# A grouped 1x1 convolution on one core: an in-place ring of five slots of 104 columns in place of four of 128

## The chip, the core and the metric

The kernel runs on one core of one Trainium2 chip. The metric is the device time of the program in microseconds (us). A core has a matmul engine (TensorE, PE in the profile; its weight loads are shown apart as PEld), VectorE (DVE), ScalarE (ACT), GpSimd (POOL) and SyncE (SP), each with an instruction queue of its own, and 16 DMA engines that all transfers share. SyncE and ScalarE issue transfers that the hardware unrolls; GpSimd issues transfers that its software unrolls.

## The reference

A 1x1 grouped convolution over 512 x 512 pixels of 192 channels: four groups of 48 channels, each with its own 48 x 48 matrix. Input, weights and output are bf16.

```
x: [1, 512, 512, 192]   w: [1, 1, 4, 48, 48]
xg  = x.reshape(1, 512, 512, 4, 48)
out = einsum('bhwgc,gcd->bhwgd', xg, w[0, 0]).reshape(1, 512, 512, 192)
```

So each pixel's 192 values are multiplied by a block-diagonal 192 x 192 matrix. 100.7 MB are read and 100.7 MB written.

## The kernel before

**Layout.** A "column" is one pixel in each of the 128 partitions, 384 bytes per partition. The input comes into a ring in SBUF, `ring`, of `COLS` columns (512 here, four slots of `SLOT` = 128). The work is in place: results are written over the inputs, and the slot is then stored to the output from the ring. A "group" is 4 columns, a "pair" two groups. There are 529 groups, in 265 pairs (the last has one group).

**Pieces.** `plan_pieces` cuts the image into pieces. The first slot comes in four pieces of growing size (`HEAD`), the others in one piece of `SLOT` columns each; the last slot has what is left, 68 columns here. Two slots, those whose numbers are in `SHARED_AT`, end in a shared piece of 64 columns (`WIDE`) that uses only 60 of the 128 rows and is loaded and stored by GpSimd, in row ranges that leave out one of the 16 DMA engines. Before such transfers GpSimd issues tiny ones (`cur`) that move its place among the engines.

**Who does what.**

- SyncE loads the pieces in order (line 248). Before each it waits until the stores of the columns that the piece takes over have landed (`wait_free`). After the first piece it issues the load of the weights (line 250).
- GpSimd waits for each piece's landing and then adds the piece's pairs to the semaphore `ready` (line 233). It also issues the shared pieces' loads, two pieces ahead, and their stores.
- TensorE first spreads the weights into the block-diagonal matrix `wt` by 10 small matmuls (line 262). Then, for every pair, it transposes the two groups (12 transposes, line 285, into `xT_ps`) and, one pair behind, multiplies the transposed groups by `wt` (12 matmuls, line 299, into `o_ps`). It waits on `ready` at the pairs where a piece may begin. The loop over pairs is a hardware loop whose body is two slots (`LOOP` groups, 64 here); the ring address of each group comes from registers, six a group, computed from a base that depends on the turn (line 269). What is left after whole turns is written out straight.
- VectorE copies each pair's transposed data from PSUM to SBUF (line 336).
- ScalarE copies each group's result from PSUM back over the group's columns in the ring (line 362) and issues the store of a piece as soon as its last group and one more are done (line 356). The stores of the last three slots are cut in halves, and the last slot's store in `LAST_PARTS`.

**Order.** Each engine's order is written out by hand; nothing is planned by cost. PSUM has four banks for transposed groups (`NXP`) and four for results (`NOB`), SBUF two buffers for transposed pairs (`NXS`).

Of the kernel before, what the change touches and what calls it, by code (L numbers as in the profile page):

```python
# [22 lines left out]
ESHIFT = 112  # L23
ECOLS = 272

SLOT = 128
COLS = 4 * SLOT
COL = 2 * C
HEAD = (8, 24, 32, 64)
LATE = 3  # L30
LAST_PARTS = (28, 16, 12, 12)
LOOP = 2 * SLOT // 4
SHARED_AT = (4, 10)
RING = 16766
SYNC, POOL = 0, 1
WIDE = 64
# [27 lines left out]
class Piece:  # L64

    def __init__(self, i, slot, g0, size, shares, pix):
        self.i, self.slot, self.size = i, slot, size
        self.at = 4 * g0 % COLS
        self.g0, self.g1 = g0, g0 + size // 4
# [5 lines left out]
        self.pix_end = pix  # L75
        assert size % 4 == 0 and self.at + size <= COLS

# [4 lines left out]
def plan_pieces(npix):  # L82
    few = sum(rows * cols for _, rows, _, cols, _ in SHARED)
    at = list(SHARED_AT)
    if npix < len(at) * few + 128 * SLOT * (1 + at[-1]):
        at = []
# [3 lines left out]
    while cols:  # L90
        if n in at:
            parts = [(SLOT - WIDE, None), (WIDE, SHARED)]
        elif n == 0 and cols >= SLOT:
            parts = [(s, None) for s in HEAD]
        else:
            parts = [(min(SLOT, cols), None)]
        for s, shares in parts:
# [8 lines left out]
def bass_standalone__grouped__vision_kernel(nc, x, w, out):  # L106
# [9 lines left out]
    LP = LOOP // 2  # L116
# [5 lines left out]
    wv = w.rearrange("a b g c d -> c (a b g) d")  # L122

    def groups(pair):
        return range(2 * pair, min(2 * pair + 2, NG))

    def span(c0, c1, r0=0, r1=128):
        return ring[r0:r1, c0 * COL:c1 * COL].bitcast(BF16)
# [13 lines left out]
    for p in pieces:  # L142
        late = pieces[-1].slot - p.slot
        half = p.size // 8 * 4
        parts = (p.size,)
        if p is pieces[-1] and p.size == sum(LAST_PARTS):
            parts = LAST_PARTS
        elif p.full and late < LATE and half:
            parts = (p.size - half, half)
        c = 0  # L150
# [7 lines left out]
    with ExitStack() as es:  # L158
        block = es.enter_context(nc.Block())
        ring = es.enter_context(nc.sbuf_tensor("ring", [128, COLS * COL], U8))  # L160
        xT_sb = [es.enter_context(nc.sbuf_tensor(f"xT_sb{i}", [128, 4 * UC], BF16)) for i in range(NXS)]
        ident = es.enter_context(nc.sbuf_tensor("ident", [128, 128], BF16))
        esel = es.enter_context(nc.sbuf_tensor("esel", [CG, ECOLS], BF16))
        w_sb = es.enter_context(nc.sbuf_tensor("w_sb", [CG, GROUPS, CG], BF16))
# [4 lines left out]
        def sem(name):  # L169
            return es.enter_context(nc.semaphore(name))  # L170
# [7 lines left out]
        w_sem, id_sem, e_sem, wb_sem, wc_sem = (sem(s) for s in ("w_sem", "id_sem", "e_sem", "wb_sem", "wc_sem"))  # L178
# [4 lines left out]
        def columns(g):  # L183
            c = 4 * g % COLS
            return span(c, c + 4)

        def wait_stored(wq, i):
            p = stores[i][0]
            wq.wait(st_sem[i], 16 * len(p.on(SYNC)))
            if p in pooled:  # L190
                wq.wait(ps_sem[p], pool_val[p])

        def wait_free(wq, p):
            lap = COLS // 4
            for i in sorted({store_of[g - lap] for g in range(p.g0, p.g1) if g >= lap}):
                wait_stored(wq, i)
# [45 lines left out]
        @block.sync  # L242
        def _(sp):
            wq = Waiter(sp)
            for p in pieces:
                wait_free(wq, p)
                for _, dram, sbuf in transfers(xf, p, SYNC):
                    sp.dma_start(sbuf, dram).then_inc(ld_sem[p.i], 16)  # L248
                if p.i == 0:
                    sp.dma_start(w_sb[:], wv).then_inc(w_sem, 16)  # L250

        @block.tensor
        def _(pe):

            def build_weights():
                pe.wait_ge(e_sem, 1)
                pe.wait_ge(w_sem, 16)
                last = None
                for (tc, r, g, c0_) in WBLOCKS:
                    s0 = ESHIFT - r  # L260
                    col = WOFF[tc] + c0_
                    last = pe.matmul(o_ps[:, NOB - 1, col:col + CG], lhsT=esel[:, s0:s0 + 128],  # L262
                                     rhs=w_sb[:, g, :], start=True, stop=True, skip_group_check=True)
                last.then_inc(wb_sem, 1)

            def addresses(base, g):
                regs = [pe.alloc_register(f"at{g}_{i}") for i in range(6)]
                for i, r in enumerate(regs):
                    pe.reg_add(r, base, RING + 4 * g * COL + i * 256)
                return [pe.snap(r, donate=True, min_val=RING, max_val=RING + COLS * COL - 256,  # L270
                                guaranteed_mod_val=0, out_of_modulus=2) - RING for r in regs]

            def transposes(j, gs, base=None):
                if j % LP in starts:
                    n = min((s - j) % LP or LP for s in starts)
                    pe.wait_ge(ready, min(j + n, NP - first[0]))
                last = None
                for g in gs:
                    if base is None:
                        ats = [4 * g % COLS * COL + i * 256 for i in range(6)]  # L280
                    else:
                        ats = addresses(base, g % LOOP)
                    for i, at in enumerate(ats):
                        xs = ring[:, bass.ds(at, 256)].bitcast(BF16)
                        last = pe.transpose(xT_ps[:, g % NXP, i * 128:(i + 1) * 128], xs, ident[:])  # L285
                last.then_inc(t_left, 1)

            def matmuls(j, gs):
                pe.wait_ge(e_left, j + 1)
                for g in gs:  # L290
                    xs = xT_sb[j % NXS][:, g % 2 * 2 * UC:(g % 2 + 1) * 2 * UC]
                    pe.wait_ge(o_left, g + 1)
                    last = None
                    for ul in range(2):
                        v = 2 * g + ul
                        for tc in range(3):
                            i = ul * 3 + tc
                            c0_, c1_ = COLR[tc]
                            last = pe.matmul(o_ps[:, v % NOB, c0_:c1_], lhsT=xs[:, i * 128:(i + 1) * 128],  # L299
                                             rhs=wt[:, WOFF[tc]:WOFF[tc] + (c1_ - c0_)],  # L300
                                             start=(tc == 0), stop=(tc == 2), skip_group_check=True)
                    last.then_inc(mm_done, 1)

            first = [0]
            build_weights()
            pe.wait_ge(id_sem, 1)
            pe.sem_inc(o_left, 2)
            transposes(0, groups(0))
            pe.wait_ge(wc_sem, 1)
            if turns_of_loop:  # L310
                with pe.Fori(0, turns_of_loop) as turn:
                    here = pe.snap((turn & 1) * (LOOP * 4 * COL))
                    there = pe.snap(((turn + 1) & 1) * (LOOP * 4 * COL))
                    for j in range(LP):
                        transposes(j + 1, range(2 * j + 2, 2 * j + 4), here if j + 1 < LP else there)
                        matmuls(j, range(2 * j, 2 * j + 2))
                    pe.sem_inc(ready, -LP)
                    pe.sem_inc(e_left, -LP)
                    pe.sem_inc(o_left, -LOOP)
            first[0] = LP * turns_of_loop  # L320
            for j in range(NP - first[0]):
                if j + 1 < NP - first[0]:
                    transposes(j + 1, groups(first[0] + j + 1))
                matmuls(j, [g - 2 * first[0] for g in groups(first[0] + j)])
# [22 lines left out]
        @block.scalar  # L347
        def _(act):
            wq = Waiter(act)
            todo = list(stores)  # L350

            def store():
                i = len(stores) - len(todo)
                p, c0, c1, g1 = todo.pop(0)
                for _, dram, sbuf in transfers(of, p, SYNC, c0, c1):
                    act.dma_start(dram, sbuf).then_inc(st_sem[i], 16)

            for g in range(NG):
                wq.wait(mm_done, g + 1)
                v = 2 * g  # L360
                dst = columns(g).rearrange("p (u c) -> p u c", u=2)
                act.copy(dst, o_ps[:, v % NOB:v % NOB + 2, 0:UC]).then_inc(o_left, 1)  # L362
                while todo and todo[0][3] < g:
                    store()
            while todo:
                act.wait_ge(o_left, todo[0][3] - LOOP * turns_of_loop + 2)
                store()
            for i in range(len(stores)):
                wait_stored(wq, i)
# [28 lines left out]
```

## Time and profile before

| | |
|---|---|
| Three timed runs | 478.95, 482.16, 483.46 us; median 482.16 |
| The profiled execution | 477.98 us, span 476.3 us |
| Granted TensorE clock, mean | 0.979 |
| TensorE busy | 438.8 us (92%), its weight loads 397.6 us (83%) |
| ScalarE busy | 399.0 us (84%) |
| VectorE busy | 254.0 us (53%) |
| GpSimd busy | 10.0 us (2%) |
| DMA | 7565 packets, 201.52 MB, mean 423 GB/s over the span |
| Loads by SyncE | 20, of 384 to 6144 KB |
| Stores by ScalarE | 25, of 384 to 6144 KB |
| Chain that ended last | DMA 57%, TensorE 38% |

The profile is of one execution. Times inside it count from the first instruction of the program, so the span is a little less than the execution's own time. "DMA share" is the mean busy share of the 16 DMA engines. The first wait for the weights' load ends at 4.24 us; the transposes of the first pair start at 4.73 us and those of the second, which need the second piece, at 9.32 us.

### The profile page before, as it was taken

The numbers are of one execution on the slowest core, as the hardware profiler recorded it, in microseconds if no ns is written. First come the engines' busy times: TensorE is split into PE (matmuls) and PEld (weight loads), VectorE is DVE, ScalarE is ACT, GpSimd is POOL, SyncE is SP. The second block draws the span as 40 slices with busy tenths as digits, with TensorE's granted clock in tenths as the row PEclk, the third lists the DMA queues.
The fourth block names the chain that finished last, engine by engine and source line by source line (L and its number), as shares of the span: only waits on it lengthen the run. The fifth ranks groups of instructions, "written<-read, shape, count | busy, mean of one in ns | idle before, by whom it ended". The sixth has DMA issues, their size and how long they took to land.

```text
span 476.3 us, 14542 instructions
## 1 busy us (share of the span) xinstructions
PE 438.8 (92%) x6358; PEld 397.6 (83%) x6358; DVE 254.0 (53%) x266; ACT 399.0 (84%) x530; POOL 10.0 (2%) x23
## 2 busy tenths in 40 slices
PE   3999889999999999999799999999899998989993
PEld 3988778898888989888798889889798977979982
DVE  2555545655556555565355655555555553545651
ACT  1888879999899989999599998989898995968993
POOL 1000000100001000000010000010000000000000
PEclk9999999999999999999799999999999998989997
DMA  8999999999999999999999999999999999999997
GB/s 285 436 421 441 433 418 427 440 431 444 425 433 429 420 431 436 452 413 450 421 434 425 414 433 425 438 429 423 438 436 433 434 429 433 433 424 421 431 412 292
DMA packets 7565, 201.52 MB, mean 423 GB/s; under 512 B 1553, under 2 KB 1553, under 8 KB 2193
## 3 DMA queue, kind: packets, MB, share of 16 engines
q1 hardware_dynamic: 3088, 97.73, 48.1%
q10 hardware_dynamic: 3600, 97.72, 47.8%
q0 software_dynamic: 864, 5.91, 3.0%
q8 instruction: 8, 0.13, 0.1%
q14 instruction: 5, 0.03, 0.0%
HBM read 100.69 MB, written 100.66 MB: 423 GB/s over the span
## 4 chain that ended last, share of the span: by engine, by line
DMA 57%; PE 38%; issue 2%; ACT 1%; SPq 0%; POOL 0%; POOLq 0%
DMA ring<-in_x_dram 32%; DMA out_dram<-ring 24%; PE o_ps L299 22%; PE xT_ps L285 16%; ACT ring L362 1%; SPq L248 0%; POOL cur L218 0%; POOL out_dram L220 0%; SPq L250 0%; POOLq L233 0%; SPq L54 0%
## 5 line engine op out<-in xcount | busy, mean ns | idle before, releaser
L362 ACT CAST ring<-o_ps 128x768 bf16<-128x768 f32 x529 | 397.7, 802 | 69.5 <-PE o_ps L299 61.7
L336 DVE COPY xT_sb<-xT_ps 128x1536 bf16<-128x1536 bf16 x265 | 253.3, 956 | 208.0 <-PE xT_ps L285 208.0
L299 PE MATMUL o_ps<-wt,xT_sb 128*128 128x144 bf16 (+1 forms) x3174 | 296.5, 235 | 8.1 <-issue 3.6
L299 PEld LDWEIGHTS o_ps<-wt,xT_sb 128*128 128x128 bf16 x3174 | 215.2, 99 | 46.3 <-ACT ring L362 29.9
L285 PE MATMUL xT_ps<-ident,ring 128*128 128x128 bf16 x3174 | 225.0, 221 | 17.4 <-POOLq L233 14.6
L285 PEld LDWEIGHTS xT_ps<-ident,ring 128*128 (+1 forms) x3174 | 193.6, 99 | 20.2 <-issue 19.9
L218 POOL DMA_DIRECT2D cur<-in_x_dram x7 | 4.2, 596 | 306.5 <-DMA out_dram<-ring 169.4
L262 PE MATMUL o_ps<-w_sb,esel 48*128 48x48 bf16 x10 | 0.6, 210 | 4.2 <-DMA w_sb<-in_w_dram 4.2
L262 PEld LDWEIGHTS o_ps<-w_sb,esel 48*128 48x128 bf16 x10 | 0.5, 112 | 4.2 <-issue 4.2
L330 DVE CAST wt<-o_ps 128x480 bf16<-128x480 f32 x1 | 0.7, 658 | 4.8 <-PE o_ps L262 4.8
L220 POOL DMA_DIRECT2D ring<-in_x_dram x4 | 2.3, 582 | 0.0
L220 POOL DMA_DIRECT2D out_dram<-ring x4 | 2.3, 576 | 0.0
L362 ACT ACT_TABLE_LOAD x1 | 1.3, 1283 | 0.8 <-PEq L383 0.8
L204 POOL TENSOR_SCALAR_AFFINE_SELECT esel<-esel 48x272 bf16<-48x272 bf16 x1 | 0.4, 402 | 0.0
L201 POOL MEMSET esel<- 48x272 bf16 x1 | 0.3, 317 | 0.3 <-POOLq L383 0.3
L208 POOL TENSOR_SCALAR_AFFINE_SELECT ident<-ident 128x128 bf16<-128x128 bf16 x1 | 0.3, 282 | 0.0
L202 POOL MEMSET ident<- 128x128 bf16 x1 | 0.2, 198 | 0.0
L383 POOL MEMSET const-float32-0.0<- 128x1 f32 x1 | 0.1, 98 | 0.3 <-issue 0.3
L383 POOL MEMSET const-bfloat16-1.0<- 128x1 bf16 x1 | 0.1, 101 | 0.0
L383 POOL MEMSET const-uint8-127<- 128x1 uint8 x1 | 0.1, 101 | 0.0
L383 POOL MEMSET const-float32-1.0<- 128x1 f32 x1 | 0.1, 98 | 0.0
## 6 DMA issues: line engine op xcount, KB each, us to landing
ring<-in_x_dram SPq DMA_DIRECT2D x13, 6144.0 KB, 39.7
out_dram<-ring ACTq DMA_DIRECT2D x11, 6144.0 KB, 35.0
out_dram<-ring ACTq DMA_DIRECT2D x7, 3072.0 KB, 31.8
ring<-in_x_dram SPq DMA_DIRECT2D x3, 3072.0 KB, 22.1
ring<-in_x_dram SPq DMA_DIRECT2D x1, 3264.0 KB, 34.0
ring<-in_x_dram POOLq DMA_DIRECT2D x2, 1056.0 KB, 25.4
out_dram<-ring POOLq DMA_DIRECT2D x2, 1056.0 KB, 28.9
ring<-in_x_dram SPq DMA_DIRECT2D x1, 1536.0 KB, 11.0
```

The lines of the kernel that those rows point to most:

```text
L201: gp.memset(esel[:], 1.0).then_inc(p0_sem, 1)
L204: gp.affine_select(out=esel[:], in_=esel[:], pattern=[[-1, ECOLS]], compare_op=AluOpType.is_equal, fill=0.0, base=ESHIFT, channel_multipli ...
L208: gp.affine_select(out=ident[:], in_=ident[:], pattern=[[-1, 128]], compare_op=AluOpType.is_equal, fill=0.0, base=0, channel_multiplier=1) ...
L218: gp.dma_start(cur[0:n, turns[0]], few).then_inc(cur_sem, 16)
L220: gp.dma_start(*((sbuf, dram) if inward else (dram, sbuf))).then_inc(done, 16)
L262: last = pe.matmul(o_ps[:, NOB - 1, col:col + CG], lhsT=esel[:, s0:s0 + 128], rhs=w_sb[:, g, :], start=True, stop=True, skip_group_check=True)
L285: last = pe.transpose(xT_ps[:, g % NXP, i * 128:(i + 1) * 128], xs, ident[:])
L299: last = pe.matmul(o_ps[:, v % NOB, c0_:c1_], lhsT=xs[:, i * 128:(i + 1) * 128], rhs=wt[:, WOFF[tc]:WOFF[tc] + (c1_ - c0_)], start=(tc == ...
L330: dve.tensor_copy(wt[:], o_ps[:, NOB - 1, 0:WCOLS]).then_inc(wc_sem, 1)
L336: dve.tensor_copy(xT_sb[pair % NXS][:, 0:n * 2 * UC].rearrange("p (g c) -> p g c", g=n), xT_ps[:, b0:b0 + n, 0:2 * UC]).then_inc(e_left, 1)
L362: act.copy(dst, o_ps[:, v % NOB:v % NOB + 2, 0:UC]).then_inc(o_left, 1)
L383: nc = _bacc.Bacc("TRN2", target_bir_lowering=False, num_devices=1)
```

## The change

- `SLOT` goes from 128 to 104 and the ring from four slots to five, so from 512 to 520 columns. There are then 20 full slots and a last one of 36 columns.
- `HEAD`'s last piece goes from 64 to 40 columns, the last slot's store parts are 16, 12 and 8 columns, and the shared pieces stand in slots 6 and 13 instead of 4 and 10.
- TensorE's loop body is still two slots, now 52 groups. As two slots no longer divide the ring evenly, a turn's base isn't one of two values: three slot bases (the third for the pair that is transposed ahead of the next turn) are computed at the head of a turn, each by modulo five. There are ten turns where there were eight, and 5 pairs after them where there were 9.
- The weights' load is issued by ScalarE, as its first instruction, in place of SyncE.

```diff
-SLOT = 128
-COLS = 4 * SLOT
+SLOT = 104
+SLOTS = 5
+COLS = SLOTS * SLOT
 COL = 2 * C
-HEAD = (8, 24, 32, 64)
+HEAD = (8, 24, 32, 40)
 LATE = 3
-LAST_PARTS = (28, 16, 12, 12)
+LAST_PARTS = (16, 12, 8)
 LOOP = 2 * SLOT // 4
-SHARED_AT = (4, 10)
+SHARED_AT = (6, 13)
...
@@ block.sync
                     sp.dma_start(sbuf, dram).then_inc(ld_sem[p.i], 16)
-                if p.i == 0:
-                    sp.dma_start(w_sb[:], wv).then_inc(w_sem, 16)
@@ block.tensor
-            def addresses(base, g):
-                regs = [pe.alloc_register(f"at{g}_{i}") for i in range(6)]
+            uses = [0]
+
+            def addresses(base, c):
+                regs = [pe.alloc_register(f"at{uses[0]}_{i}") for i in range(6)]
+                uses[0] += 1
                 for i, r in enumerate(regs):
-                    pe.reg_add(r, base, RING + 4 * g * COL + i * 256)
+                    pe.reg_add(r, base, RING + c * COL + i * 256)
...
-            def transposes(j, gs, base=None):
+            def transposes(j, gs, bases=None):
...
-                        ats = addresses(base, g % LOOP)
+                        ats = addresses(bases[4 * g // SLOT], 4 * g % SLOT)
...
                 with pe.Fori(0, turns_of_loop) as turn:
-                    here = pe.snap((turn & 1) * (LOOP * 4 * COL))
-                    there = pe.snap(((turn + 1) & 1) * (LOOP * 4 * COL))
+                    bases = [pe.snap((turn * 2 + k) % SLOTS * (SLOT * COL)) for k in range(3)]
                     for j in range(LP):
-                        transposes(j + 1, range(2 * j + 2, 2 * j + 4), here if j + 1 < LP else there)
+                        transposes(j + 1, range(2 * j + 2, 2 * j + 4), bases)
                         matmuls(j, range(2 * j, 2 * j + 2))
@@ block.scalar
             wq = Waiter(act)
+            act.dma_start(w_sb[:], wv).then_inc(w_sem, 16)
             todo = list(stores)
```

More of the change, by code (lines that the diff above doesn't have):

```diff
@@ L278, in transposes @@
                 for g in gs:
-                    if base is None:
+                    if bases is None:
                         ats = [4 * g % COLS * COL + i * 256 for i in range(6)]
                     else:
-                        ats = addresses(base, g % LOOP)
+                        ats = addresses(bases[4 * g // SLOT], 4 * g % SLOT)
                     for i, at in enumerate(ats):
```

## The prediction

> **What bounds the kernel now.** I read the page's tables by slice first, then the DMA queues, then a table by stages, then TensorE's idle time.
>
> ```profile
> PEclk9999999999999999999799999999999998989997
> DMA  8999999999999999999999999999999999999997
> GB/s 285 436 421 441 433 418 427 440 431 444 425 433 429 420 431 436 452 413 450 421 434 425 414 433 425 438 429 423 438 436 433 434 429 433 433 424 421 431 412 292
> ...
> q1 hardware_dynamic: 3088, 97.73, 48.1%
> q10 hardware_dynamic: 3600, 97.72, 47.8%
> q0 software_dynamic: 864, 5.91, 3.0%
> ```
>
> See that the 16 DMA engines are full in every slice but the first and the last, at about 430 GB/s. The shares of the queues (with 0.1% for instructions) make 99.0%: 471.5 us of the 476.3 us span are packet time of the mean engine. The answer by stages says where the rest is:
>
> ```profile
> 0.00:12.00 12.00, 4.63 (x45) 4.32 (x46) 2.57 (x3) 1.69 (x2) 1.31 (x8) 1.00 0.81 286
> 12.00:60.00 48.00, 44.45 (x647) 40.04 (x646) 25.69 (x27) 40.77 (x55) 0.00 (x0) 1.00 1.01 430
> ...
> 240.00:300.00 60.00, 58.69 (x874) 53.33 (x872) 34.60 (x37) 54.57 (x73) 0.34 (x1) 1.00 1.00 427
> ...
> 450.00:464.00 14.00, 13.80 (x203) 12.23 (x201) 8.36 (x9) 12.62 (x18) 0.00 (x0) 1.00 0.97 414
> 464.00:477.00 13.00, 3.93 (x53) 3.11 (x50) 1.77 (x3) 5.01 (x7) 0.00 (x0) 0.74 0.67 275
> ```
>
> Columns: busy PE, weight load, DVE, ACT, POOL, then clock, DMA share, GB/s. DMA stands idle for 19% of 12 us at the start (2.3 us), 0.4 us at 450 to 464 and, to the span's end at 476.3, 12.3 - 13 x 0.67 = 3.6 us in the tail. In between its share is 1.00.
>
> The second resource is TensorE, and it has little to spare:
>
> ```profile
> PE xT_ps L285 <- POOLq L233: 14.6, 8, 3.3
> ...
> 122.07 0.83 PE L285 MATMUL xT_ps<-ident,ring 128*128 128x128 bf16 x12 [0.69 <-issue]
> ...
> 228.73 1.44 PE L285 MATMUL xT_ps<-ident,ring 128*128 128x128 bf16 x12 [2.87 <-POOLq L233]
> 229.97 1.80 PE L299 MATMUL o_ps<-wt,xT_sb 128*128 128x144 bf16 x12
> 231.57 1.48 PE L285 MATMUL xT_ps<-ident,ring 128*128 128x128 bf16 x12
> ```
>
> The first line is the list of waits (TensorE waits for a landed load, told by POOL), the others its timeline. After the startup TensorE waited for loads six times, at 225.9, 310.5, 337.4, 364.9, 391.9 and 422.9. Take from three of them the 0.65 us that a turn's head costs anyway, and 8.7 us are left. After three of them it runs cold: from one pair's transposes to the next 2.84 us (228.73 to 231.57) where 1.63 is usual; by such differences 5.0 us in all. So TensorE's slack is 13.7 us in the span, and the end is set by DMA: mean packet time, start and tail.
>
> **The change, part by part.** Base: the profiled execution, 477.98 us (span 476.3, 1.7 around it). The three timed runs are 1.0, 4.2 and 5.5 us above it.
>
> *Weights from ScalarE's queue.* Removed: one issue on SyncE between the first and second load (1.23, 0.42 us), so the seven loads behind it start up to 0.48 us earlier (1.71 to 1.23). DMA is short of work just there (0.81), so I take -0.4, with ends 0 and -0.5. On ScalarE the issue stands beside a table load (0.81 to 2.09); at worst it comes behind that, 0.9 us later than now. TensorE's weight build (4.24) and first transposes then slip, covered by the wait for the second load that ends at 9.32: the weights are cast at 5.49, 3.8 us before it. Cost 0; without cover 0.9.
>
> *More, smaller transfers.* The 1988 full columns and two shared pieces stay, so bytes stay 201.52 MB. Pieces: 20 full slots and 36 columns, where 16 and 68 were. SyncE's loads go from 20 to 24, ScalarE's stores from 25 to 28: seven transfers of 128 rows and 16 completions, 1008 packets. Price of a packet: q10 takes 0.478 x 476.3 x 16 / 97.72 = 37.3 us per MB; q0's 5.91 MB at that rate are 220 us, its share is 229, so 8 us over 864 packets, some 9.6 ns. The trace's packet records say the same: 49152 bytes took 1815 ns, 24576 took 912, 12288 took 460, that is 9 ns and 0.0367 ns a byte. 1008 x 9.6 / 16 = +0.6 us on every engine. Rows of 39936 bytes are not in the trace; rows of 26112 (968 ns) and 10752 (404 ns) lie on the same line, so I take the line. Three more issues on ScalarE (0.34 us each) lie beside its copies; it is idle for 69.5 us.
>
> *Ring of 5 x 104.* 520 columns instead of 512, in finer steps: a load waits for a store of 104 columns, not 128. It can only fill DMA gaps, and between 12 and 450 there are none: even from 91.7 to 105.7, when no load of SyncE was under way, the share was 1.01 (88 to 106). Value 0; ends -0.4 (the gap at 450 to 464) and 0.
>
> *TensorE's loop.* Ten turns of 52 groups for eight of 64: two more heads, 2 x 0.67 = +1.3. Three bases by modulo five replace two by mask: by the expressions up to 11 register operations a turn where the trace has 5; one takes 0.04 us and they start 0.09 to 0.13 apart, so +0.1 (one more at the head, others beside the array) to +0.8 a turn, if the modulo is one operation. That makes +2.3 to +9.3 us for TensorE. In the first turn its stalls of 1.25 (50.27) and 1.53 (59.79) stand beside 16 KB instruction fetches; the shorter body should have one fewer, -1.3. Sum +1 to +8: inside the 13.7 of slack, so 0 on the end. The modulo's price is not in the trace; with three operations for each it would be some 20, over the slack by 6.
>
> The Trainium skill ("Runtime: NRT & Kernel Launch", Instruction fetch mechanics) says that a taken branch out of the fetched window forces a fetch before execution goes on, which speaks against more turns. The trace has heads of 0.69, 0.65 and 0.64 and no fetch between 70 and 450; so this body is not refetched, and the same section's 128 KiB for TensorE fits that. By the rule two more heads would stall some 1.5 us each, 3 us more, still under the slack.
>
> *Tail.* The last store falls from 12 to 8 columns, the work behind the last wait for a load from 49 groups (424.9 on) to 35. Now the last issue is at 469.36 and lands 6.6 us later: 1.4 is its own transfer, 2.2 the fixed part (the first load: 384 KB landed 3.1 after issue, 0.9 of it transfer), so 3.0 is queue. Compute is that much early, and a shorter one gains nothing unless it becomes late. 0, ends -1.5 (the fast engines' idle) and 0.
>
> Sum: -0.4 + 0.6 = +0.2, so 478.2 on the profile's own base, and 482.4 if the timed runs keep their 4.2. I forecast no change, 481.5: nearly all of that excess kept, since no row says what makes it.
>
> **Rivals.**
>
> *A, faster: the excess is ring.* If timed executions lose those 4.2 us to waits for a slot that this execution was spared, finer slots take them away. The floor is 471.5 of packets, some 2.0 before the first (the first stage has 1.8 us without any) and 1.7 around the span, 475.2; with the spread of the engines in the tail, about 477. For it: a chain that is 57% DMA, store to load to store through four slots. Against: no gap in the middle. 0.22.
>
> *B, slower: turn heads on TensorE.* It decides once its added 1 to 8 us exceed its slack. That is 13.7 here, but if the timed excess is a lower clock, the slack is already spent: then 482.2 + 8 = 490. For it: clock at 0.7 in one slice, and cold pairs at twice the time. Against: the same cold pairs come only after waits for DMA. 0.12.
>
> *C, slower: every transfer pays its fixed part.* Seven more at 2.2 us (row above) are 15 us if nothing lies beside them: 497. The Trainium skill ("DMA: Bandwidth & Descriptors", Anatomy of one DMA) has about 2 us fixed per transfer. Against: the share of 1.00 over 45 transfers, so they lie beside each other. 0.03.
>
> *D, it does not do what it says:* the weights' issue sits behind the table load and the loads start no earlier in effect; 0.4 back, 482. 0.03.
>
> **The numbers.** Forecast 0.60; A 0.22, B 0.12, C 0.03, D 0.03. 1% (4.8 us) is about what a measurement here can tell, as the three runs lie 4.5 apart. Faster A, 0.22; same forecast and D, 0.63; slower B and C, 0.15. The range goes from the floor, 475.2, to just under B's full price, 489: left out are C, B's upper part and a little below the floor.
>
> **What would show it.** Right: DMA shares of 1.00 from 12 to 450 again, the second load issued at 1.2, loads x24 and stores x28 with queue shares together near 99%, TensorE's waits for landed loads shorter by about what its heads grew. A: the span falls below 475 with less DMA idle at the tail. B: waits for loads gone, heads well over 1 us, DMA share under 0.97 in the middle. C: dips of DMA at each piece. I would be wrong if rows of 39936 bytes took more than 1.48 us (the line), or if DMA stood idle in the middle of timed executions, which no profile of one execution can tell.

## The result, and the profile after

The changed kernel takes 477.03 us (median, 475.51 to 483.48) where the kernel before takes 480.80 (478.27 to 484.47, timed again on the same chip). The ratio is 0.9913, 95% interval 0.9890 to 0.9936: 0.9% faster, just inside the 1% that was called no change, but clear of 1. Ratios, here and below, are taken from fast runs alone, those within 1.5% of the fastest of their kernel, so they differ a little from the quotient of the medians.

The profiled executions do not show this: span 476.3 and time 477.98 before, span 476.2 and time 478.20 after. The profiled execution before lies below all twenty timed runs of its kernel, the one after among the upper ones of its own. What a single trace can and cannot tell is half of what follows: each profile below, too, is of one execution.

DMA by slices and the DMA queues on the page after:

```profile
DMA  8999999999999999999999999999999999999996
GB/s 345 430 432 426 427 436 438 429 418 424 423 413 429 430 443 426 425 438 433 433 429 430 434 437 424 436 429 437 423 404 437 429 423 426 423 438 439 413 431 284
...
q1 hardware_dynamic: 3456, 97.72, 48.1%
q10 hardware_dynamic: 4240, 97.73, 47.9%
q0 software_dynamic: 864, 5.91, 3.0%
```

The engines are full again from end to end. Two things differ: the first slice moves 345 GB/s, not 285 (60 x 11.9 us = 0.71 MB, 1.7 us of DMA at 430 GB/s; in the profiles below, late starts move 301 to 323 and early ones 342 to 364), and the two main queues carry 7696 packets, not 6688, for 96.0% of the span, not 95.9%. By stages (busy PE, weight load, DVE, ACT, POOL, clock, DMA share, GB/s):

```profile
0.00:12.00 12.00, 6.58 (x69) 6.24 (x70) 3.11 (x4) 3.01 (x4) 1.31 (x8) 1.00 0.86 344
12.00:60.00 48.00, 43.49 (x642) 39.18 (x640) 25.31 (x27) 40.36 (x54) 0.00 (x0) 1.00 1.02 433
...
240.00:300.00 60.00, 58.76 (x873) 53.34 (x872) 34.92 (x37) 54.44 (x73) 2.27 (x4) 1.00 1.01 432
...
450.00:464.00 14.00, 11.30 (x158) 9.60 (x155) 6.30 (x7) 11.67 (x16) 0.00 (x0) 1.00 1.00 428
464.00:477.00 13.00, 0.00 (x0) 0.00 (x0) 0.00 (x0) 0.00 (x0) 0.00 (x0) 0.54 0.65 272
```

The last row is the new thing: all compute is over before 464, where TensorE and ScalarE still worked before; DMA alone runs the last 13 us. From 450 to 464 DMA has no gap (1.00, before 0.97). From TensorE's waits and its timeline:

```profile
PE xT_ps L287 <- POOLq L234: 10.1, 5, 3.1
...
7.37 1.46 PE L287 MATMUL xT_ps<-ident,ring 128*128 128x128 bf16 x12 [1.14 <-POOLq L234]
...
142.44 0.84 PE L287 MATMUL xT_ps<-ident,ring 128*128 128x128 bf16 x12 [0.60 <-issue]
```

The second pair's transposes start at 7.37 us, 1.95 earlier than before. A turn's head with three modulos costs 0.60 us, not more than the 0.65 to 0.69 with two masks. Waits for loads fall from 14.6 to 10.1 us; 2.0 of these 4.5 us are the second pair's (3.13 before, 1.14 now).

### The profile page after: what moved, and what is told of

Its sections match the earlier page's. It is cut to its first block, busy times and chain, and to the rows that moved or that the text cites. A ratio compares the mean times of both kernels' runs of the same rounds, so it can differ in the third digit from the quotient of the medians.

```text
span 476.2 us, 14571 instructions
## 1 busy us (share of the span) xinstructions
PE 435.7 (92%) x6358; PEld 394.8 (83%) x6358; DVE 254.1 (53%) x266; ACT 398.7 (84%) x530; POOL 10.0 (2%) x23
## 4 chain that ended last, share of the span: by engine, by line
PE 65%; DMA 22%; another core or an unknown queue 7%; issue 2%; ACT 1%; SPq 0%; POOL 0%; POOLq 0%
PE o_ps L301 38%; PE xT_ps L287 27%; DMA ring<-in_x_dram 13%; DMA out_dram<-ring 8%; ACT ring L364 1%; SPq L249 0%; POOL cur L219 0%; POOL out_dram L221 0%; POOLq L234 0%; SPq L55 0%
## 5 line engine op out<-in xcount | busy, mean ns | idle before, releaser
L287 PE MATMUL xT_ps<-ident,ring 128*128 128x128 bf16 x3174 | 223.6, 221 | 14.5 <-POOLq L234 10.1
```

## The experiments

Ratios are to the kernel before, timed beside each. The two theories at the outset: **S**, the gain is the start (the weights' load moved); **R**, it is the ring.

**The two parts apart, and TensorE's slack.** The first kernel has the weights' move alone:

```diff
-                if p.i == 0:
-                    sp.dma_start(w_sb[:], wv).then_inc(w_sem, 16)
...
+            act.dma_start(w_sb[:], wv).then_inc(w_sem, 16)
```

> The kernel before with one edit: the weights' load is ScalarE's first instruction and no longer stands between SyncE's first two loads; ring, loop and store parts as before. In the profile of the changed kernel the second pair's transposes start at 7.37 us where they started at 9.32, and the first slice moves 345 GB/s where it moved 285 (60 x 11.9 us = 0.71 MB, 1.7 us of DMA). Theory S (the gain of 0.9% is the start): ratio 0.991 to 0.997, 1.7 to 4 us of 481, and the same early start. Theory R (the gain is the ring): the start comes early as well, but the ratio lies between 0.997 and 1.001.

The second undoes just this in the changed kernel.

> The changed kernel with the weights' load back on SyncE behind the first piece; ring of five slots, loop, shared pieces and store parts as changed. Theory S: ratio to the kernel before 0.998 to 1.002, since the ring only adds seven transfers (0.6 us). Theory R: 0.991 to 0.996. If both parts give about half, 0.995 to 0.997.

Weights alone: 479.40 us, 0.9953 (0.9922 to 0.9984). Ring alone: 478.38 us, 0.9949 (0.9917 to 0.9980). Both intervals end below 1, so each part gains. By the middle values they are worth about half each, and their product, 0.990, agrees with the whole. Neither theory alone fits well, though not by much: S wanted the ring alone at 0.998 or more, which is just where its interval ends, and R the weights alone at 0.997 or more, which its interval still holds. The start shows in the profile with the weights alone: 360 GB/s in the first slice, and the second pair at 7.30:

```profile
7.30 1.44 PE L283 MATMUL xT_ps<-ident,ring 128*128 128x128 bf16 x12 [1.16 <-POOLq L233]
```

Two kernels give TensorE more to do:

```diff
-                    for i, at in enumerate(ats):
+                    for i, at in list(enumerate(ats)) * (2 if bases is not None and j in (5, 15) else 1):
```

(`base` in place of `bases` in the kernel before.)

> The changed kernel with the transposes of two pairs a turn done twice (the same data into the same place): 24 more transposes a turn, 1.34 us, 13.4 us of TensorE over ten turns. If DMA sets the end, as the tail of its profile says (last copy at 462, last store landing at 476), the time stays within 1 us of the changed kernel: ratio 0.990 to 0.994. If TensorE has become the bound, 13 us more: ratio near 1.02.

> The kernel before with the same double transposes, two pairs a turn in eight turns: 10.7 us more of TensorE. If its end is set by DMA with 13.7 us of slack, ratio 0.999 to 1.004. If the timed executions of the four-slot ring are lengthened by waits that go through TensorE (load, compute, store, load), much of the 10.7 us shows: 1.008 to 1.022, and then five slots, which do not show theirs, have gained by slack.

Five slots with 13.4 us more, by the estimate: 476.91 us, 0.9928 (0.9896 to 0.9960). Four slots with 10.7 us more: 481.96, 1.0006 (0.9980 to 1.0032). So TensorE's work is not the bound in the timed executions of either kernel, and rival B falls. In the profiles TensorE's busy time grows by less than the estimate, from 435.7 to 446.4 us with five slots (span 474.2) and from 438.8 to 444.3 with four (span 476.8); its idle time took the work.

**What of the ring gives its half?** Three kernels timed together: the changed one with four slots (`SLOTS = 4`, a ring of 416 columns), the changed one with no stores cut at the end (`LATE = 0`, `LAST_PARTS = (36,)`), and a finer ring:

```diff
-SLOT = 104
-SLOTS = 5
+SLOT = 72
+SLOTS = 7
...
-HEAD = (8, 24, 32, 40)
+HEAD = (8, 24, 40)
...
-LAST_PARTS = (16, 12, 8)
+LAST_PARTS = (12, 8, 8)
...
-SHARED_AT = (6, 13)
+SHARED_AT = (9, 19)
```

> The changed kernel with four slots of 104 columns, a ring of 416: pieces, transfers, shared pieces, store parts and start are those of the changed kernel, only the fifth slot is gone. Theory R1 (the ring's half of the gain, 0.5%, is the fifth slot: loads run further ahead): ratio 0.995 or more, with longer waits of TensorE for loads. Theory R2 (it is the smaller pieces or the shorter last slot): the changed kernel's 0.991.

> The changed kernel with no stores cut at the end: the last three slots are stored in one transfer each, the last one its 36 columns at once; five transfers fewer. If the last copies stand well ahead of DMA, as at 462 against 476, nothing is lost, and the ratio stays at 0.991 (five transfers fewer are 0.4 us). If the short last store makes the ring's half of the gain, 0.994 or more.

> Seven slots of 72 columns, 504 in all, first pieces of 8, 24 and 40, last store parts 12, 8 and 8 of a last slot of 28, shared pieces in slots 9 and 19. Theory R3 (finer steps of the ring are worth something by themselves): 0.990 or less. Theory R1 (what counts is how many columns lie between load and store): 504 is less than 512, so the ring's half is lost, 0.995. More transfers (some 20) cost 20 x 144 x 9.6 ns / 16 = 1.7 us, 0.4%, in any case.

Four slots of 104: 479.98 us, 0.9979 (0.9949 to 1.0010): without the fifth slot the ring's half is gone, though pieces, last slot and store parts are those of the changed kernel. Plain tail: 476.13 us, 0.9898 (0.9859 to 0.9937): the cut stores at the end are worth nothing here. Seven slots of 72: 477.69 us, 0.9930 (0.9906 to 0.9954), with 0.4% of it the price of more transfers by the estimate above (summed from the packet records, the packet time of the mean engine is 472.7 us, 1.1 us more than before). So 504 columns seem to keep the ring's half, or most of it, and it is not a matter of 520 against 512; the interval alone still holds 0.995, where that half would be lost, and the kernel with all loads halved, below, is the better evidence.

Where the four short slots can lose time is plain in the profile of that kernel. It is of the second longest of twelve executions (483.07 us, the median is 479.98), so it shows more of the loss than is usual (stages as above):

```profile
420.00:450.00 30.00, 26.83 (x378) 24.52 (x376) 14.73 (x17) 23.64 (x32) 0.00 (x0) 0.94 0.99 420
450.00:464.00 14.00, 13.86 (x210) 12.69 (x209) 8.34 (x9) 12.81 (x18) 0.00 (x0) 1.00 0.87 370
464.00:477.00 13.00, 8.33 (x114) 6.86 (x111) 4.39 (x5) 8.99 (x12) 0.00 (x0) 0.97 0.72 297
```

Now compute is late: TensorE waits longer for loads (19.2 us in ten waits, 5.1 the longest), works on past 464, and the DMA engines, with all loads done, run dry between its stores (0.87, 0.72). In this execution the time is lost at the end, not in the middle, where the share is 1.00 in this kernel too.

**The end alone.** If so, it should help four slots of 128 to bring the last two full slots in halves, so that TensorE can start on them sooner. On top of the weights' move:

```diff
             parts = [(min(SLOT, cols), None)]
+            if SLOT < cols < 3 * SLOT:
+                parts = [(SLOT // 2, None)] * 2
```

`LATE` is 0 in this and the two after it, which here leaves the stores of these two slots in halves as they were. The next halves every slot after the first (`if SLOT < cols:`).

> Four slots of 128 as before, the weights from ScalarE, and one more edit: the last two full slots come in two loads of 64 columns each (their stores were halves already). Theory T (the ring's half of the gain is made at the end: TensorE's last wait for a load then has less work behind it, 33 or 49 groups with the wait ending earlier, and DMA isn't left idle after 450): ratio 0.990 to 0.993, the last copies end before 465. Theory M (it is made by finer steps all along the run): as with the weights alone, 0.994 to 0.997.

> Four slots of 128 as before, the weights from ScalarE, every slot after the first in two pieces of 64 columns, each loaded, announced and stored by itself: eight steps of 64 in the same 512 columns. Some 20 transfers more, 1.7 us (0.4%). Theories T and M: ratio 0.991 to 0.995 (the ring's half of the gain less the transfers). If the gain needs the 520 columns or the loop of two short slots: 0.998 or more (weights alone plus the transfers).

The first was a surprise: 484.76 us, 1.0067 (1.0039 to 1.0096), 1.1% above the weights alone. Theory T in this form fell, and theory M's range was missed as well. The second: 476.22 us, 0.9889 (0.9857 to 0.9920), its six runs within 0.42 us: 512 columns in steps of 64 have all of the gain, so neither the 520 columns nor the loop of two short slots is needed. It is the lowest ratio of all here and below both kernels' medians, though its interval overlaps that of the changed kernel.

The profile with the last loads halved: TensorE waits for the last load at 460, ScalarE's last store is issued at 476.79, and DMA stands idle for 37% of the stretch from 450 to 464: the loads are ending and the next stores are not computed yet. Timeline, stages, and the DMA issues (KB each, us to landing):

```profile
460.21 0.83 PE L285 MATMUL xT_ps<-ident,ring 128*128 128x128 bf16 x12 [1.42 <-POOLq L235]
...
476.79 0.34 ACTq L357 DMA_DIRECT2D out_dram<-ring  x1
...
450.00:464.00 14.00, 12.44 (x186) 11.27 (x185) 7.36 (x8) 11.51 (x17) 0.00 (x0) 1.00 0.63 270
...
ring<-in_x_dram SPq DMA_DIRECT2D x1, 3264.0 KB, 57.9
```

The last load took 57.9 us from issue to landing, against 34.0 in the kernel before; it was issued earlier, at 401.9 us and not at 408.1, so a late issue is not the reason. The trace's packet records suggest why. From 380 to 390 us the engines moved 54 load rows of 24576 bytes and 54 store rows of 49152. That is what comes out if an engine with both queues full takes a row of each in turn: the bytes then go by the rows' sizes, 1.33 MB for loads and 2.65 MB for stores. In the kernel before the same 10 us had 46 load rows and 43 store rows of the same 49152 bytes. The stretches beside it are less even, from 51 load rows against 62 store rows (410 to 420) to 104 against 32 (390 to 400); from 360 to 420 the loads had 9.8 MB of 25.2, 39%, where the kernel before gave them 49%. Halving only the loads had halved their rows, and cut the loads' share. That can be tried: cut every 128-column store in two as well.

```diff
-        elif p.full and late < LATE and half:
+        elif p.full and p.size == SLOT:
```

> The kernel with the last two slots' loads halved (1.007), and every 128-column store cut in two halves, issued one after the other, so that all stores have rows of 24576 bytes. In the trace of the kernel without this, the engines took a row of each queue in turn: from 380 to 390 us 54 load rows of 24576 bytes and 54 store rows of 49152, a third of the bytes for loads, and the last load landed at 459. Theory A (rows in turn make the halved loads late): with equal rows the last load lands by 445, the last copies end before 466, ratio 0.989 to 0.994. Theory B (halving the last loads is bad for another reason): still 1.003 or more, the last load near 459.

477.10 us, 0.9920 (0.9891 to 0.9948): from slower than before to as fast as the changed kernel, by the stores' cut alone. Theory A holds. From 380 to 390 us it has 81 load rows and 94 store rows, all of 24576 bytes; the last load takes 26.0 us and lands at 436, and the last store is issued 18 us before the end of the span:

```profile
456.38 0.34 ACTq L357 DMA_DIRECT2D out_dram<-ring  x1
...
450.00:464.00 14.00, 4.92 (x66) 3.89 (x62) 2.47 (x3) 5.98 (x8) 0.00 (x0) 0.82 1.01 433
...
ring<-in_x_dram SPq DMA_DIRECT2D x1, 3264.0 KB, 26.0
```

Loads and stores are not cut alike in this kernel: up to its last two slots, loads have rows of 49152 bytes and stores of 24576 (64 load rows against 49 store rows from 340 to 350 us, about 2.6 times the bytes). The turns by row favour the loads there, and its compute ends further ahead than in any other.

The last stores of the kernel before, of the changed one and of the ring alone, and the ring alone's last stages (of two stores in a line, the second is issued at 462.87 and 462.50):

```profile
469.36 0.34 ACTq L356 DMA_DIRECT2D out_dram<-ring  x1
...
462.05 1.62 ACTq L358 DMA_DIRECT2D out_dram<-ring  x2
...
461.68 1.64 ACTq L359 DMA_DIRECT2D out_dram<-ring  x2
...
465.00:470.00 5.00, 0.00 (x0) 0.00 (x0) 0.00 (x0) 0.00 (x0) 0.00 (x0) 0.50 0.97 413
470.00:475.00 5.00, 0.00 (x0) 0.00 (x0) 0.00 (x0) 0.00 (x0) 0.00 (x0) 0.50 0.62 255
```

Put beside each other, the distance from the last store's issue to the end of the span is 5.8 to 7.6 us in the five kernels without the ring's half of the gain (last loads halved 5.8, before 6.9, four slots of 104 7.1, four slots with more TensorE 7.5, weights alone 7.6). It is 9.9 to 18.3 in all that have it: 9.9 with five slots and more TensorE, 12.5 all halved, 13.3 changed, 14.0 seven slots, 14.7 plain tail, 16.9 ring alone, 18.3 stores halved too (and 12.2 and 14.4 in the two below that ran once).

An early last store does not make every execution quick. The ring alone was profiled in the longest of its twelve, 481.38 us: its compute is over at 462.5, 16.9 us before the end, and by the packet records the 16 engines are all at work until about 471, as in the changed kernel. Then they run out one by one: at 475 us four are still busy (two in the changed kernel), and the last store packet ends at 478.3 (475.4). This spread of the engines is a second thing that lengthens the end; no run here was made to change it.

**Why the start is worth more than the issue.** A tiny load between SyncE's first two, in the changed kernel:

```diff
                     sp.dma_start(sbuf, dram).then_inc(ld_sem[p.i], 16)
+                if p.i == 0:
+                    few = xf[0:16, 0:128].rearrange("p (a b) -> p a b", a=2)[:, :, 0:32]
+                    sp.dma_start(cur[0:16, 15], few).then_inc(x_sem, 16)
...
```

> The changed kernel with a tiny load (16 rows of two 64-byte pieces, 32 descriptors) issued by SyncE between its first two loads, where the kernel before had the weights (192 pieces of 96 bytes). If the later issue alone (0.42 us) made the slow start, the second pair's transposes start at 7.8 us or later and the first slice moves about 325 GB/s. If the 192 small pieces made it, they start at 7.3 to 7.8 and the slice stays near 345. If any transfer between the two costs the 2 us, 9.3.

And a wait in that place that issues nothing (`sp.wait_ge(e_sem, 1)`):

> The changed kernel, where SyncE waits between its first two loads for GpSimd's first mask (done at about 1.7 us in every profile) and issues nothing there: the second load is issued at about 1.75 us, as in the kernel before and with the tiny transfer, with no transfer between. If the later issue makes the slow start, the second pair's transposes start at 9.2 to 9.9 us as in those two, and the first slice moves 285 to 325 GB/s. If a transfer between the two makes it, they start at 7.3 to 8.0 and the slice moves some 340.

With the tiny load the second pair starts at 9.91 us (305 GB/s in the first slice), with the wait alone at 9.46 (301):

```profile
9.91 0.39 PE L292 MATMUL xT_ps<-ident,ring 128*128 128x128 bf16 x2 [3.73 <-POOLq L235]
```

```profile
9.46 0.82 PE L289 MATMUL xT_ps<-ident,ring 128*128 128x128 bf16 x6 [3.23 <-POOLq L234]
```

Neither the 192 small pieces nor any transfer between is needed: that the second load is issued at 1.72 to 1.74 us and not at 1.24 makes it land some 2 us later. In the packet records its 128 rows of 9216 bytes take 399 ns in the mean in both, as against 352 to 372 in the changed kernel, with the weights alone, and with all pieces halved; a row of that size takes 350 in the mean later in the run. More of the delay comes from idle engines. The first rows of the second load start at 3.0 to 3.4 us in every profile, but from 3.7 to 4.9 us only 10 to 14 of the 16 engines are at work, in the mean, in all five profiles with the later issue, and 15.7 or more in the nine with the earlier one: some engines get their rows late. The early starts were not all alike: with the plain tail, whose start is the changed kernel's, the second pair came at 8.57. Why half a microsecond costs four times itself there stays open. What the late start costs the whole time was not measured apart: these two kernels ran once each (477.59 and 478.87 us).

## Why the prediction was right or wrong

No change was forecast, and 0.9% was measured, inside the 1% by a little. That was partly luck. The forecast was 0.7 us down, from 482.16 to 481.5; measured were 3.8 us down, from 480.80 to 477.03. Two terms hold the difference: the weights, put at -0.4, and the ring, put at 0, came out at about 2.4 us each. A little more, and the change would have been over 1%.

*What bounds the kernel:* held. DMA shares are 1.00 in the middle in all profiles but for single stages at 0.98 or 0.99, and 10.7 to 13.4 us more TensorE work, by the estimate, show in neither kernel's time.

*Weights, -0.4:* the sign held, the size did not. The step took the gain for the earlier issue, 0.48 us; the profile has 1.7 us more DMA work done in the first slice (the share of the first 12 us rises by 0.6 us, from 0.81 to 0.86, and rows take less time: the third load's, of 12288 bytes, 462 ns in the mean where they took 550), and the part alone gave 0.47% of 481, 2.3 us (0.8 to 3.8). The part on cover held: the build of the weights still ends its wait at 4.28 us, and nothing waited for it.

*Packets, +0.6:* in line with the two profiles, not shown by them. There are 1008 more packets on the two queues and 0.1% more of the span, 0.5 us; but in five profiles with the same 7696 packets the packet time of the mean engine, summed from the records, lies between 471.2 and 472.7 us, around the 471.6 before. Rows of 39936 bytes lie on the line (median 1476 ns; 1490 in the mean, by some longer ones).

*Ring, 0 with ends -0.4 and 0:* this term failed. It was read off the DMA shares of one execution and, in the middle, rightly; but the loss, as far as the profiles show it, is at the end, when only stores are left and compute may be late, and the profiled execution had been a quick one. The ring alone gave 0.51%, 2.5 us (1.0 to 4.0). Rival A had this ("the excess is ring", about 477 us) at 0.22; its time is the measured one, for half of the reason, and its sign, a span under 475 us, is met by 10 of the 20 timed executions but not by the profiled one. My forecast of 481.5 kept the timed runs' excess because no row said what made it; that was a reason to doubt, not to keep.

*Loop, +1 to +8 for TensorE, 0 on the end:* 0 on the end held; the cost was overrated. The compiler turned the three bases into three fused register operations of 0.05 to 0.10 us at the head, so ten heads of 0.60 stand against eight of 0.66: +0.7 us. The sign that waits for loads would shrink by what the heads grew did not come: they fell by 4.5 us. No 16 KB fetch of instructions (queue q8) starts between 57 and 461 us, as between 68 and 457 before; the prediction's "no fetch between 70 and 450" overlooks three of 8 KB on q14 (at 156, 268 and 376; now at 158, 257 and 369), beside which TensorE's timeline before shows no stall.

*Tail, 0:* the reading that compute was 3.0 us early held for the profiled execution. That an earlier last store gains nothing seems not to hold in general: 3 us is small enough to be used up when a load comes late, and the changed kernel has about 13 us between the last issue and the end. The cut of the last slot's store, which the term was about, is worth nothing, as the plain tail shows.

*The other rivals:* B fell with the two kernels that give TensorE more to do. C fell: with seven more transfers the packet time of the mean engine is 472.2 us (471.6 before), and the share by stage stays at 0.99 to 1.02 from 12 to 464 us. (The section of the Trainium skill that the prediction names there describes transfers that GpSimd issues; these seven are issued by SyncE and ScalarE.) D fell: ScalarE issues the weights' load at 0.82 us, before its table load, and the second load starts earlier in effect.

What is not shown: no profile of a typical, longer execution of the kernel before exists here. That its lost 2.5 us are the late tail is argued from the two kernels in which DMA is seen to run dry at the end (four slots of 104, last loads halved) and from the two that make compute early and win (all halved, stores halved too). The profile of the ring alone, long with an early last store, shows that the late tail is not all that lengthens an execution.

## What to carry to other kernels

This DMA-bound kernel, which streams through a ring in place, lost little in the middle but could lose at the end, when stores alone are left. In such a kernel read there how far ahead of the end the last store is issued, and see whether finer pieces widen that; here 10 us and more went with the gain, 8 us and less without. Cut no load finer than the stores beside it: here, when both queues were full, the one with the longer rows took more of the bandwidth. And one profiled execution whose time lies under all the timed ones can't show what the others lose.

## What was not expected of the hardware

With two full queues the DMA engines took rows of both in turn, whatever the rows' sizes (54 of 24576 bytes against 54 of 49152 in 10 us), so the halved loads had a third of the bytes there, and 39% over 60 us. The records do not name the engine, so that each engine alternates is inferred from the counts. The Trainium skill ("DMA: Bandwidth & Descriptors", Queues, rings and completion order) has the engines take turns between queues packet by packet, a packet being several descriptors; that they take turns agrees, but here a turn was, by these counts, one row. That bytes are then shared by row size cost 1.1%, which the kernel with the stores halved too got back.

The second load issued 0.5 us later landed 2 us later (the second pair starts at 9.3 to 9.9 us against 7.1 to 8.6), with or without a transfer between, and 2 to 6 of the 16 engines stood idle meanwhile, in the mean; why is open.
